# A linear-attention block beside an FFN on one core: kv products in row pairs, smaller first pieces, a split last tile and a new order

## The chip, the cores and the metric

The kernel runs on one core of one Trainium2 chip. The metric is the device time of one execution in microseconds: the median of five runs. Lower is better. Inputs and outputs lie in the chip's main memory and are bf16; products are accumulated in fp32 in PSUM (eight banks).

## The reference

With S = 2048 tokens, D = 448, H = 16 heads of 28 and F = 1792, cut to what matters:

```python
xn = layernorm(x)                                   # A_x; both branches read it
q, k, v = heads(xn @ wqkv)
phi = lambda p: concat(softmax(p), softmax(-p))     # per head, 28 + 28 features
phi_q, phi_k = phi(q @ w_phi), phi(k @ w_phi)
kv = einsum("sf,sd->fd", phi_k, v)                  # per head: sum over all tokens
z  = phi_k.sum(tokens)
o  = (phi_q @ kv) / (phi_q . z + 1e-6)
out = x + merge(o) @ wo + silu(xn @ w1) @ w2
```

## The kernel before

The tokens are cut into 16 tiles of 128. The whole program is recorded first as a list of operations with their data dependencies, and then ordered for each engine by a planner in `schedule()`, from estimated durations and landing times. TensorE's order is nearly written out by hand: the text `PLAN` (from `aF3@4`) fixes the order of its operations from the first chunk of tokens on, and the planner only places the other engines' work and the DMA issues around it. All waits are semaphores that follow from the dependencies.

The work runs in these stages.

- Front. x comes in pieces of one, one, two, four, four and four tiles on SyncE's queue, with pieces of w1 between them (`load_x`, `load_w1`, `load_rows4`). While they come, 38 matmuls on ones keep TensorE busy. `ln_tile(t)` computes mean and variance on DVE, the root of the variance on ACT (tiles 0 to 3) or POOL (later tiles) and the normalised tile `xn` on DVE. Tiles 0 to 3 are transposed by TensorE (`tr0` to `tr3`) and evicted by ACT or DVE; from tile 4 on, two tiles at a time are transposed by a DMA on SyncE's queue (`xnT_dma5`, `xnT_dma7` and so on). The weights of q and k are transposed in the same queue (`wT_dma0` to `wT_dma7`) and multiplied with w_phi on TensorE (`fold_mms`, the words `f2` and `f0` of the plan), so that q and k come out with w_phi applied.
- FFN, first half. `F0` to `F27` are blocks of two 128-row pieces of the hidden layer by 512 tokens; a Silu on ACT evicts two banks at once into `hT`. Blocks 0 to 6 need tiles 0 to 3, blocks 7 to 13 need tiles 4 to 7, and so on. The first three blocks (`head`) are computed tile by tile as the tiles arrive.
- v, k and q blocks of two tiles each. A k or q block has two exponentials on ACT, sums and reciprocals on DVE and a multiply on POOL (`phi_k`, `phi_q`); phi_q is transposed by DMA.
- kv. `kv(ts)` multiplies phi_k with v (and a column of ones for z), head pairs at a time: eight matmuls of 58 columns for each tile, all 16 tiles accumulated in bank 7. `kvm()` masks the result into `KVm` on DVE.
- Attention and output. `U` words multiply phi_q with `KVm`; DVE divides, and a DMA transposes the result. `Y` and `F` words with a count are pieces of the second FFN product (14 matmuls for a tile), `W`, `R`, `r` and `E` add the output projection; `out_ev` adds the residual and sends the tile out.

F, v, k and q blocks have a contraction of 448, which is three and a half times 128. They run in 64-row mode: each matmul uses half of the array's rows, two of them form a pair that writes two banks, and a block has seven pairs. In the plan `a` stands for the first half of a block (three pairs), `b` for the second (four pairs, with the row halves exchanged between the two banks, then the eviction). `@4` is the first of the block's banks. Everything else, kv, fold, U, Y and most of the output projection, uses all 128 rows.

SyncE's queue carries nearly all DMAs in one order, part of which is fixed by `chain(...)`: `wT_dma0` to `wT_dma3`, `xnT_dma5`, `wT_dma4`, `xnT_dma7`, `wT_dma5` to `wT_dma7`, the other token tiles, w2 and wo. The loads of x for tiles 8 to 15 stand before them.

The lines that the change touches most:

```python
pe_mms([(banks[KVB][wide(c), c * 2 * DA:(c + 1) * 2 * DA], ek(t)[:, 0, c * KP:c * KP + wide(c).stop],
         vaug[:, t, 2 * c:2 * c + 2, :]...,
         t == 0 and c == 0, t == NT - 1) for t in ts for c in range(CC)], "kv_mm", ...)
```

Of the kernel before, what the change touches and what calls it, by code (L numbers as in the profile page):

```python
# [140 lines left out]
class _Prog:  # L141
# [68 lines left out]
    def dma(self, fn, xfer, reads=(), writes=(), name="", out_slot=None, eng="sp", issue=480.0, lat=1700.0):  # L210
        o = self.op(eng, issue, fn, reads, writes, name=name)
        o.is_dma = True
        o.xfer = xfer
        o.lat = lat
        o.out_slot = out_slot
        return o

    def schedule(self):
# [21 lines left out]
        eng_free = {e: 800.0 if e == "sp" else 0.0 for e in ENGINES}  # L240
# [93 lines left out]
PLAN = """aF3@4 aF4@0 bF3 aF5@2 av2@6 bF4 bv2 bF5 aF6@0 bF6 av0@4 bv0 aF7@0 aF8@2 aF10@4 bF8 bF10 bF7 f2@26 aF11@4 aF13@0 bF11  # L334
bF13 f0@26 aF9@4 aF12@0 bF9 av4@2 ak0@6 bv4 bF12 bk0 av6@4 av8@2 ak4@0 bv8 bk4 bv6 av14@6 ak2@2 bv14 bk2 av12@0 ak6@4
bv12 bk6 ak8@6 av10@2 ak10@0 bv10 bk10 bk8 ak12@2 ak14@4 bk12 bk14 aq4@0 Y0@6:3 Y0:2 K0-6 bq4 aq6@4 K6-8 bq6 aq0@2 aq8@0
bq0 bq8 aF15@4 Y0:9 K8-12 bF15 aF19@2 aF14@0 bF19 bF14 aF17@5 s4 aF18@3 bF17 bF18 K12-16 aF16@5 aF21@2 aF24@0 bF21 bF16
bF24 M s6 aF27@2 aF26@4 bF27 aF22@0 bF26 bF22 aF20@6 aq2@2 bF20 aF23@0 aF25@4 bF23 bF25 bq2 U4 s8 F4@1:10 U9@0 s0 aq12@6
aq14@4 aq10@2 s2 bq12 bq10 bq14 F4:3 F4:1 F9@0:10 F8@3:3 F8:3 s10 W4 U8 s12 F8:6 Y1@4:14 F9:4 W9 U2 U0@5 F2@2:6 F2:8
F8:2 U7@6 U12@5 W8 Y3@4:9 Y3:5 W2 s14 W0@5 F7@4:9 F7:1 U1 F7:4 W7 R0,2 R8,7 R4,9 F10@6:5 U6@5 U10 F10:9 U3@3 F5@4:14  # L340
U13@2 F15@51:8 U15 F15:6 F12@2:5 F12:9 U14 F6@0:5 W12 E15 U5 F13@3:11 F6:9 F14@7:5 F13:2 F13:1 U11@1 W5 W3@5 r12 W13
F14:9 W14 r14 W6 W1@2 W10 R3,6,13,1,5,10 F11@1:7 F11:6 F11:1 W11 r11"""


def bass_parallel_sum__linear_kernel_hedgehog__dense_activation_silu__prompt_kernel(
# [13 lines left out]
    G = 4  # L359
# [16 lines left out]
    with es:  # L376
# [39 lines left out]
        oT_sb = vflat[:, NO * 512:(NO + NQ) * 512].rearrange("p (n g c) -> p n g c", n=NQ, g=G)  # L416
        KVm = sb("KVm", [KP, CC, 2, DA], BF16)
# [79 lines left out]

        memset(ones_bf[:], 1.0, 128, "ones")
# [6 lines left out]
        act(warm_act[:], ones_bf[:, 0:4], ACTF.Sqrt, 4, "warm_act", table="sqrt")  # L505
# [19 lines left out]
        def load(dst, src, name, eng="sp", lat=1700.0):  # L525
            n = 2
            for _, cnt in list(dst.ap):
                n *= cnt
            P.dma(lambda e: e.dma_start(out=dst, in_=src), n / 280.0, writes=[dst], name=name, eng=eng, lat=lat)  # L529

# [3 lines left out]
        def load_rows4(dst, src, c0, c1, name, lat=1700.0):  # L534
            load(dst[:, 0:3, :], src[0:KF, c0:c1].rearrange("(k p) f -> p k f", p=128), name, lat=lat)
            load(dst[:, 3, :], src[D - 128:D, c0:c1], name, lat=lat)

        def load_w1(c0, c1, lat=1700.0):
            load_rows4(w1_sb[:, :, c0:c1], B_w1, c0, c1, "w1", lat)

        load(Wp[:], A_w_phi.rearrange("(g hl) d f -> (hl d) g f", g=G), "wphi", eng="act", lat=3000.0)
# [3 lines left out]
        load_w1(0, 512)  # L545
        load_w1(512, 1024)
        load_x(4, 8)
        load_w1(1024, FF)
# [8 lines left out]
        def dma_t(dst, src, xfer, name, issue=1235.0, **kw):  # L557
            o = P.dma(lambda e: e.dma_start_transpose(out=dst, in_=src), xfer, lat=650.0, reads=[src] if kw.pop("sbuf", True) else [],
                      writes=[dst], name=name, issue=issue if xfer < 1500.0 else 2000.0, **kw)
            o.crowd = 1  # L560
# [10 lines left out]
        def fold_loads():  # L571
            for a in range(8):
                dma_t(wT_sb[:, a, :], A_wqkv[:, a * KP:a * KP + 128], 600.0, f"wT_dma{a}", (1600.0, 1400.0, 1780.0, 3280.0)[a] if a < 4 else 1300.0, sbuf=False)
# [22 lines left out]
        def ln_tile(t):  # L596
            xs = x_sb[:, t, :]
            sl = t % NXN
            P.op("dve", 590, lambda e: e.bn_stats(st6[:, t, :], xs), reads=[xs], writes=[st6[:, t, :]], name=f"bnst{t}", okeys_w=["ln"])  # L599
            P.op("dve", 170, lambda e: e.bn_aggr(mv[:, t, :], st6[:, t, :]), reads=[st6[:, t, :]], writes=[mv[:, t, :]], name=f"bnag{t}",  # L600
                 okeys_w=["ln"])
            if t < 4:
                P.op("act", 220, lambda e: e.activation(ve[:, t:t + 1], mv[:, t, 1:2], ACTF.Sqrt, bias=epst[:]),
                     reads=[mv[:, t, 1:2], epst[:]], writes=[ve[:, t:t + 1]], name=f"ve{t}", table="sqrt", okeys_r=["sq"])
                P.op("dve", 120, lambda e: e.reciprocal(rstd[:, t:t + 1], ve[:, t:t + 1]),
                     reads=[ve[:, t:t + 1]], writes=[rstd[:, t:t + 1]], name=f"rstd{t}")
            else:
                P.op("pool", 200, lambda e: e.tensor_scalar(ve[:, t:t + 1], mv[:, t, 1:2], EPS_LN, None, ALU.add),
                     reads=[mv[:, t, 1:2]], writes=[ve[:, t:t + 1]], name=f"ve{t}")
                P.op("pool", 570, lambda e: e.tensor_tensor(rstd[:, t:t + 1], ve[:, t:t + 1], neghalf[:], ALU.pow),  # L610
                     reads=[ve[:, t:t + 1], neghalf[:]], writes=[rstd[:, t:t + 1]], name=f"rstd{t}")

            def norm(dst, c0, c1, dur):
                P.op("dve", dur, lambda e: e.tensor_scalar(dst, x_sb[:, t, c0:c1], mv[:, t, 0:1], rstd[:, t:t + 1], ALU.subtract, ALU.mult),  # L614
                     reads=[xs, mv[:, t, 0:1], rstd[:, t:t + 1]], writes=[dst], name=f"xn{t}")

            if t < XN_DMA0:
                norm(xn_sb[:, sl, 0:D], 0, D, 390)
            else:
                norm(xn_sb[:, sl, 0:KF], 0, KF, 370)  # L620
                norm(xn_sb[:, sl, KF:512], D - 128, D, 250)
            dstx = xnT[:, t, :, :]
            if t >= XN_DMA0:
                if t % 2:
                    dma_t(xnT[:, t - 1:t + 1, :, :].rearrange("p i k c -> p (i k) c"),
                          xn_sb[:, sl - 1:sl + 1, :].rearrange("p i c -> p (i c)"), 1300.0, f"xnT_dma{t}", 1350.0)
                return
            tps = bank16[4 + t % 2][:, 0:512].rearrange("p (k c) -> p k c", k=4)
            transposes([(tps[:, kt, :], xn_sb[:, sl, KS[kt]:KS[kt] + 128]) for kt in range(4)], f"tr{t}")
            if t < 3:  # L630
                act(dstx, tps, ACTF.Identity, 512, f"ev{t}")
            else:
                copy(dstx, tps, 512, f"ev{t}")


# [3 lines left out]
        def pair_block(b0, width, lhs, rhs, name):  # L639
            def part(c0, c1):  # L640
                for i in range(2):
                    for n, kt in enumerate((0, 1, 2 + i)):
                        mm(banks[b0 + i][:, c0:c1], lhs(i, kt, slice(0, 128)), rhs(i, kt, slice(0, 128), c0, c1),
                           n == 0 and c0 == 0, False, name)
# [98 lines left out]
        def kv(ts):  # L743
            def wide(c):
# [3 lines left out]
            pe_mms([(banks[KVB][wide(c), c * 2 * DA:(c + 1) * 2 * DA], ek(t)[:, 0, c * KP:c * KP + wide(c).stop],  # L748
                     vaug[:, t, 2 * c:2 * c + 2, :].rearrange("p h c -> p (h c)"),
                     t == 0 and c == 0, t == NT - 1) for t in ts for c in range(CC)], "kv_mm", dur=CC * 30.0 * len(ts), keys_w=["kvbank"])  # L750
# [6 lines left out]
        def phi_q(t, pair=False):  # L757
# [8 lines left out]
            if n % 2 or not pair:  # L766
# [3 lines left out]
                      1300.0 * w, "phqT")  # L770

        def kvm():
            src = banks[KVB][0:KP, 0:2 * DA * CC].rearrange("p (c j e) -> p c j e", c=CC, j=2)
# [9 lines left out]
        def parts(bs):  # L783
            cuts = (0, D) if len(bs) == 1 else (0, 320, D)
# [55 lines left out]
        def out_ev(t, ob, addend, cs):  # L840
# [3 lines left out]
            P.dma(lambda e: e.dma_start(out=outt[:, t, cs], in_=res[:, cs]), 400.0, reads=[res[:, cs]], name="out_dma", out_slot=ob_cnt[0] % NOS,  # L844
# [35 lines left out]
        chain("bnst0 bnag0 bnst1 bnag1 rstd0 xn0 rstd1 xn1 bnst2 bnag2 bnst3 bnag3 rstd2 xn2 rstd3 xn3 ev3".split())  # L880
        chain("ev0 ve2 ev1 ve3 ev2 silu_table".split())
        chain("tr0 tr1 tr2 tr3".split())
# [8 lines left out]
        for t, fs in ((0, head[:2]), (1, head[:2]), (0, head[2:]), (1, head[2:]), (2, head), (3, head)):  # L891
            for f in fs:
                f[0](t * 128, t * 128 + 128)
# [16 lines left out]
        chain("wT_dma0 wT_dma1 wT_dma2 wT_dma3 xnT_dma5 wT_dma4 xnT_dma7 wT_dma5 wT_dma6 wT_dma7 xnT_dma9 xnT_dma11 xnT_dma13 xnT_dma15 w2 "  # L910
              "wo0 wor0 wo1 wor1".split())
        memset(phq[:, :, :, KP:128], 0.0, 400, "phq0")
        late = next(o.id for o in P.ops if o.name == "rstd15")
        ones_column(0, NEK)
        ones_column(NEK, NT)
        for o in P.ops[-2:]:
            o.odeps.add(late)
# [168 lines left out]
```

## Time and profile before

| | |
|---|---|
| median of five runs | 151.43 us (150.49 to 152.01) |
| the profiled execution | 150.49 us |
| its span in the trace | 149.2 us |
| granted TensorE clock | 1.0 in all stages |
| TensorE matmuls | 1412, busy 144.9 us |
| ScalarE (ACT), VectorE (DVE), GpSimd (POOL) busy | 70.1, 91.2, 70.9 us |

A row of the timeline has the start and the length in microseconds, the engine, the line of the kernel, the operation and the number of instructions merged in it. Matmuls are pipelined: the length of a row reaches to the modelled end of its last matmul, so the pace is read from the start of a row to the start of the next. A row of the queue (SPq, ACTq) shows the issue of a DMA, not its transfer; the time from issue to landing is a separate answer of the trace. PEld is the weight load, which overlaps the matmuls.

### The profile page before, as it was taken

To read this page: it belongs to the slowest core of one execution; us is meant where nothing else is said; L and a number is where in the kernel's file an instruction comes from. 1 tells how busy PE (TensorE), PEld (TensorE's weight loads), DVE (VectorE), ACT (ScalarE), POOL (GpSimd) and SP (SyncE) were. 2 spreads that over 40 slices of the span, in tenths; PEclk is the share of its full clock that TensorE was granted. 3 is DMA by queue.
4 is the path that set the end of the run, shared out by engine and by line. 5 is a ranking of instruction groups with operands and counts; after the bars stand their busy time and mean duration, and the time that the engine had idled before them with its cause. 6 is when DMAs were issued, how large, how long until landed. Compare 5 with 4: busy or idle time off the path is not lost.

```text
span 149.2 us, 3394 instructions
## 1 busy us (share of the span) xinstructions
PE 144.9 (97%) x1412; PEld 79.9 (54%) x1412; DVE 91.2 (61%) x186; ACT 70.1 (47%) x86; POOL 70.9 (48%) x82
## 2 busy tenths in 40 slices
PE   7899999999999999999999999999999999999993
PEld 7794435555555565464544445455555567555541
DVE  1958998940098999311995027897552874243354
ACT  3558763557999997975565585910000000000000
POOL 7108568310039999999699900899600000000000
PEclk9999999999999999999999999999999999999999
DMA  5999976999400000000099494078977646240215
GB/s 86 314 373 365 180 131 108 192 237 346 111 0 4 0 0 9 0 4 0 0 76 208 82 185 82 7 136 161 115 155 150 165 120 107 36 100 5 68 67 179
DMA packets 44352, 17.41 MB, mean 117 GB/s; under 512 B 36784, under 2 KB 43952, under 8 KB 44336
## 3 DMA queue, kind: packets, MB, share of 16 engines
q1 hardware_dynamic: 41568, 15.36, 48.4%
q10 hardware_dynamic: 2768, 1.83, 3.8%
q8 instruction: 11, 0.18, 0.5%
q14 instruction: 5, 0.04, 0.1%
HBM read 6.56 MB, written 1.84 MB: 56 GB/s over the span
## 4 chain that ended last, share of the span: by engine, by line
PE 94%; DMA 3%; SPq 1%; issue 0%; DVE 0%
PE psum L468 93%; DMA phT<-in_B_w_dram 3%; SPq L529 1%; DVE x_sb L842 0%; PE psum L483 0%
## 5 line engine op out<-in xcount | busy, mean ns | idle before, releaser
L468 PE MATMUL psum<-xnT,phT 64*128 64x512 bf16 (+1 forms) x428 | 45.2, 350 | 0.7 <-DMA phT<-in_B_w_dram 0.4
L468 PE MATMUL psum<-w_sb,hT 128*128 128x448 bf16 (+1 forms) x238 | 45.4, 342 | 0.0
L488 ACT ACTIVATE hT<-psum 128x1024 bf16<-128x1024 f32 x28 | 27.4, 1023 | 18.5 <-PE psum L468 18.5
L728 DVE TENSOR_REDUCE Rec<-Ek_sb 128x32 f32<-128x896 bf16 (+1 forms) x20 | 24.3, 1246 | 13.7 <-ACT Ek_sb L488 7.9
L468 PEld LDWEIGHTS psum<-xnT,phT 64*128 64x128 bf16 (+1 forms) x428 | 21.2, 95 | 21.4 <-ACT hT L488 0.7
L468 PEld LDWEIGHTS psum<-w_sb,hT 128*128 128x128 bf16 x238 | 21.6, 98 | 19.1 <-issue 1.5
L763 POOL TENSOR_TENSOR RA<-Ek_sb,Rec 128x896 bf16<-128x896 bf16 x16 | 26.6, 1698 | 9.1 <-ACT Ek_sb L488 7.8
L468 PE MATMUL psum<-Wqk,xnT 64*128 64x432 bf16 x224 | 22.9, 343 | 0.0
L488 ACT ACTIVATE Ek_sb<-psum 128x864 bf16<-128x864 f32 x24 | 20.3, 934 | 2.9 <-issue 2.7
L738 POOL TENSOR_TENSOR Ek_sb<-Ek_sb,Rec 128x896 bf16<-128x896 bf16 x8 | 13.3, 1696 | 11.1 <-DVE Rec L729 11.1
L820 DVE TENSOR_SCALAR den<-psum 128x16 f32<-128x16 f32 x16 | 2.5, 160 | 22.3 <-PE psum L468 22.3
L468 PEld LDWEIGHTS psum<-Wqk,xnT 64*128 64x128 bf16 x224 | 10.6, 94 | 9.5 <-ACT Ek_sb L488 0.2
L738 POOL TENSOR_TENSOR phT<-phT,Rec 128x896 bf16<-128x896 bf16 x8 | 13.3, 1693 | 0.0
L468 PE MATMUL psum<-wv,xnT 64*128 64x448 bf16 x112 | 12.9, 350 | 0.1
L599 DVE BATCH_NORM_STATS2 st<-x_sb 128x6 f32<-128x448 bf16 x16 | 9.6, 602 | 4.2 <-DMA x_sb<-in_A_x_dram 4.2
L614 DVE TENSOR_SCALAR RA<-x_sb,mv,rstd 128x384 bf16<-128x384 bf16 (+2 forms) x28 | 10.6, 414 | 1.3 <-POOL rstd L610 1.2
L468 PE MATMUL psum<-wo_sb,vaug 128*128 128x448 bf16 (+2 forms) x51 | 11.0, 342 | 0.0
L827 DVE TENSOR_TENSOR vaug<-psum,rden 128x448 bf16<-128x448 f32 x16 | 9.9, 624 | 0.4
L842 DVE TENSOR_TENSOR x_sb<-psum,x_sb 128x448 bf16<-128x448 f32 (+2 forms) x14 | 7.6, 585 | 3.8 <-PE psum L468 3.8
L729 DVE RECIPROCAL Rec<-Rec 128x32 f32<-128x32 f32 (+1 forms) x24 | 8.5, 390 | 0.1
L468 PEld LDWEIGHTS psum<-wv,xnT 64*128 64x128 bf16 x112 | 5.4, 94 | 5.5 <-PE psum L468 0.5
L488 ACT ACTIVATE vaug<-psum 128x896 bf16<-128x896 f32 x8 | 7.4, 947 | 1.6 <-PE psum L468 1.6
(49 smaller groups left out, 104.1 us busy)
## 6 DMA issues: line engine op xcount, KB each, us to landing
out_dram<-x_sb ACTq DMA_DIRECT2D x15, 112.0 KB, 1.7
w_sb<-in_B_w_dram SPq DMA_DIRECT2D x1, 1568.0 KB, 8.0
x_sb<-in_A_x_dram SPq DMA_DIRECT2D x3, 448.0 KB, 7.8
phT<-in_B_w_dram SPq DMA_DIRECT2D x2, 384.0 KB, 4.7
wo_sb<-in_A_wo_dram SPq DMA_DIRECT2D x2, 336.0 KB, 7.9
phT<-in_B_w_dram SPq DMA_DIRECT2D x1, 576.0 KB, 7.1
wv<-in_A_wqkv_dram SPq DMA_DIRECT2D x1, 336.0 KB, 7.5
phT<-in_B_w_dram SPq DMA_DIRECT2D x2, 128.0 KB, 4.8
```

Of the source, the lines that this page charges most:

```text
L468: r = e.matmul(dst, lhsT, rhs, start=st, stop=sp, skip_group_check=True)
L488: P.op("act", d_act(n), lambda e: e.activation(dst, src, func, scale=scale), reads=[src], writes=[dst], table=table, name=name, **keys)
L529: P.dma(lambda e: e.dma_start(out=dst, in_=src), n / 280.0, writes=[dst], name=name, eng=eng, lat=lat)
L599: P.op("dve", 590, lambda e: e.bn_stats(st6[:, t, :], xs), reads=[xs], writes=[st6[:, t, :]], name=f"bnst{t}", okeys_w=["ln"])
L614: P.op("dve", dur, lambda e: e.tensor_scalar(dst, x_sb[:, t, c0:c1], mv[:, t, 0:1], rstd[:, t:t + 1], ALU.subtract, ALU.mult), reads=[xs, ...
L728: P.op("dve", 50 + 967 * n, lambda e: e.tensor_reduce(R2, E4, AXL.X, ALU.add), reads=[E4], writes=[R2], name="Ssum")
L729: P.op("dve", 135 + 210 * n, lambda e: e.reciprocal(R2, R2), reads=[R2], writes=[R2], name="Rrec")
L738: P.op("pool", 1700, lambda e: e.tensor_tensor(E3, E3, Rk[:, :, None].broadcast_to([128, 32, DH]), ALU.mult), reads=[E3, Rk], writes=[E3], ...
L763: P.op("pool", 1700, lambda e: e.tensor_tensor(dst, Eq, Rq.rearrange("p (c j) -> p c j", c=CC)[:, :, :, None].broadcast_to([128, CC, 4, DH ...
L820: P.op("dve", 190, lambda e: e.tensor_scalar(den[:, uq, :], U3[:, :, DH], EPS_DEN, None, ALU.add), reads=[U3[:, :, DH]], writes=[den[:, uq ...
L827: P.op("dve", 620, lambda e: e.tensor_tensor(o3, U3[:, :, 0:DH], rden[:, uq, :, None].broadcast_to([128, H, DH]), ALU.mult), reads=[U3[:, ...
L842: P.op("dve", d_dve(cs.stop - cs.start), lambda e: e.tensor_tensor(res[:, cs], ob, addend[:, cs], ALU.add), reads=[ob, addend[:, cs]], wri ...
```

## The change

- kv: each matmul of 128 rows becomes two of 64 rows. The low half accumulates in bank 7, the high half in bank 6. `kvm()` gains two steps before the mask: ACT copies bank 6 into `kvsum`, DVE adds bank 7 to it; the mask then reads `kvsum`.
- First loads: w1's first piece has 256 columns in place of 512; its pieces for columns 256 to 767 are issued on ACT's queue behind the table load, and the rest on SyncE's queue is cut anew. The load of x for tiles 12 to 15 moves behind `xnT_dma5`; `wT_dma3` and `wT_dma4` move behind `xnT_dma7`.
- Tile 0: normalised, transposed and evicted in two halves (256 and 192 columns). The first blocks are ordered piece by piece.
- Last tile: the split of its two column parts is 224 and 224 in place of 320 and 128, and tile 15 is now the very last one (`F15@61:14 E15` ends the plan).
- `PLAN` is a new order. It starts with both halves of F3, block 12 is the first one that needs tiles 4 to 7, Y2 comes in one piece among the v and k blocks, and kv comes in groups of 4, 4, 2, 2 and 4 tiles. Estimates of issue and transfer times in the planner's calls change with it.
- The columns of ones in `Ek` are set after the last normalised tile instead of after its reciprocal root.

```diff
-PLAN = """aF3@4 aF4@0 bF3 aF5@2 av2@6 bF4 bv2 bF5 aF6@0 bF6 av0@4 bv0 aF7@0 aF8@2 aF10@4 bF8 bF10 bF7 f2@26 ...
+PLAN = """aF3@4 bF3 aF6@0 aF4@2 bF6 av2@4 bF4 av0@6 bv2 bv0 aF12@0 aF8@2 aF9@4 bF8 bF9 aF11@6 bF12 bF11 f2@24 ...
...
         load_x(0, 1)
         load_x(1, 2)
         load_x(2, 4)
-        load_w1(0, 512)
-        load_w1(512, 1024)
+        load_w1(0, 256)
+        load(w1_sb[:, 3, 256:768], B_w1[D - 128:D, 256:768], "w1_256r")
+        for c in (256, 512):
+            load(w1_sb[:, 0:3, c:c + 256], B_w1[0:KF, c:c + 256].rearrange("(k p) f -> p k f", p=128), f"w1_{c}", "act")
         load_x(4, 8)
-        load_w1(1024, FF)
+        load_w1(768, 1280)
+        load_w1(1280, FF)
...
+            if t == 0:
+                norm(xn_sb[:, sl, 0:256], 0, 256, 290, "a")
+                norm(xn_sb[:, sl, 256:D], 256, D, 275)
+                turn_over(0, 2, 4, "0a")
+                turn_over(2, 4, 5, "0")
...
-            pe_mms([(banks[KVB][wide(c), c * 2 * DA:(c + 1) * 2 * DA], ek(t)[:, 0, c * KP:c * KP + wide(c).stop],
-                     vaug[:, t, 2 * c:2 * c + 2, :].rearrange("p h c -> p (h c)"),
-                     t == 0 and c == 0, t == NT - 1) for t in ts for c in range(CC)], "kv_mm", dur=CC * 30.0 * len(ts), keys_w=["kvbank"])
+            pe_mms([(banks[KVB - i][wide(c), c * 2 * DA:(c + 1) * 2 * DA], ek(t)[r, 0, c * KP:c * KP + wide(c).stop],
+                     vaug[r, t, 2 * c:2 * c + 2, :].rearrange("p h c -> p (h c)"),
+                     t == 0 and c == 0, t == NT - 1) for t in ts for c in range(CC) for i, r in enumerate((LOW, HIGH))],
+                   "kv_mm", dur=CC * 30.0 * len(ts), keys_w=["kvbank"], mode=64, tiles=(KVB, KVB - 1))
...
         def kvm():
-            src = banks[KVB][0:KP, 0:2 * DA * CC].rearrange("p (c j e) -> p c j e", c=CC, j=2)
+            lo, hi = (banks[KVB - i][0:KP, 0:2 * DA * CC] for i in range(2))
+            P.op("act", d_act(464), lambda e: e.activation(kvsum[:], hi, ACTF.Identity), reads=[hi], writes=[kvsum[:]], name="kvhi")
+            P.op("dve", d_dve(464), lambda e: e.tensor_tensor(kvsum[:], lo, kvsum[:], ALU.add), reads=[lo, kvsum[:]], writes=[kvsum[:]], name="kvsum")
+            src = kvsum[:].rearrange("p (c j e) -> p c j e", c=CC, j=2)
...
-            cuts = (0, D) if len(bs) == 1 else (0, 320, D)
+            cuts = (0, D) if len(bs) == 1 else (0, D // 2, D)
...
-        chain("wT_dma0 wT_dma1 wT_dma2 wT_dma3 xnT_dma5 wT_dma4 xnT_dma7 wT_dma5 wT_dma6 wT_dma7 xnT_dma9 ...
+        chain("x8 wT_dma0 wT_dma1 wT_dma2 xnT_dma5 x12 xnT_dma7 wT_dma3 wT_dma4 wT_dma5 wT_dma6 wT_dma7 xnT_dma9 ...
...
-        late = next(o.id for o in P.ops if o.name == "rstd15")
+        late = max(o.id for o in P.ops if o.name == "xn15")
...
-            o.odeps.add(late)
+            o.deps.add(late)
```

## The prediction

> **What bounds the kernel now.** First the page: its busy table and its chain say which engine sets the end.
>
> ```profile
> span 149.2 us, 3394 instructions
> PE 144.9 (97%) x1412; PEld 79.9 (54%) x1412; DVE 91.2 (61%) x186; ACT 70.1 (47%) x86; POOL 70.9 (48%) x82
> PE 94%; DMA 3%; SPq 1%; issue 0%; DVE 0%
> ```
>
> TensorE is the path. A busy share can still hide slow packing, so next the chain of waits in order of time (start, length, what):
>
> ```profile
> 2.19 4.44 DMA phT<-in_B_w_dram
> ...
> 21.66 0.20 issue
> 21.85 124.98 PE psum L468 x1196
> 146.83 0.02 issue
> 146.85 0.62 DVE x_sb L842
> ```
>
> So the chain has a DMA-bound front (first useful matmul at 6.77), 125 us of unbroken matmuls, and a tail. Nothing on DVE, ACT or POOL can gain anything by itself from 22 to 147 us; only what TensorE executes, and what starts and ends its row, counts. Then the timeline of PE gives the unit prices (start, length; I read one start minus the one before, since ends overlap):
>
> ```profile
> 30.52 0.96 PE L468 MATMUL psum<-BDphi,Y_sb 112*128 112x112 bf16 x16
> 31.41 2.33 PE L468 MATMUL psum<-xnT,phT 64*128 64x512 bf16 x20
> ...
> 54.20 1.67 PE L468 MATMUL psum<-vaug,Ek_sb 128*128 128x58 bf16 x48
> 55.80 1.45 PE L468 MATMUL psum<-Wqk,xnT 64*128 64x432 bf16 x14
> 57.18 0.67 PE L468 MATMUL psum<-vaug,Ek_sb 128*128 128x58 bf16 x16
> 57.79 3.46 PE L468 MATMUL psum<-Wqk,xnT 64*128 64x432 bf16 x36
> ...
> 83.03 4.05 PE L468 MATMUL psum<-xnT,phT 64*128 64x512 bf16 x36
> 86.91 0.89 PE L468 MATMUL psum<-Wqk,xnT 64*128 64x432 bf16 x8
> ```
>
> 36 matmuls of 512 columns in 64-row mode take 86.91-83.03 = 3.88 us: 18 pairs of 0.2156 us. Two row halves cost what one matmul of 512 columns must cost at full clock, so halves run side by side. A 448-column pair is 0.189, a 432-column pair 0.183, a 128-column matmul 0.056. The kv products: 48 in 1.60 us and 16 in 0.61 us, each including one exit into 64-row mode. A mode switch: 16 fold products of 112 columns take 0.89 with their exit, 0.79 without by the same rate (0.0493 each): 0.10 us a switch. So kv is about 0.031 us per matmul, 4.0 us for all 128.
>
> **1. The front, to the first fold.** Tile 0 is normalised, transposed and evicted in two halves; w1's first piece shrinks from 512 to 256 columns, and two pieces go to ACT's queue. Before, the first matmul needed w1 (landed 2.19+4.44 = 6.63) and tile 0's eviction (5.98+0.60 = 6.58). After, x tiles 2-3 (224 KB, issued 1.73, landing 3.9 later at 5.6) still stand ahead of w1; half of the old piece should land half way from 5.6 to 6.63, 6.1. The transposes of tile 1 still come first in PE order, and DVE now spends about 0.15 more on tile 0 (two pieces in place of one of 0.40; a 128-column piece has 0.31 and overlaps its neighbour by 0.08), so tile 1's transposes end near 6.25. Start 6.3: 0.45 earlier. ACT's two issues (0.4 each) fit between its warm-up (ends 2.75) and its first variance (4.10): hidden; ACT-queue pieces share the DMA engines, and for a second piece that lands late I allow 0.15 of stalls.
>
> What follows is the same work in both orders until the first fold: 7 FFN blocks (7 pairs x 0.2156 = 1.51 each) and 2 v blocks (7 x 0.189 = 1.32). Before, this stretch also held four stalls: 0.11 (tile 2's eviction), 0.20 (a Silu that frees banks 0-1), 0.22 twice where a block's two halves are adjacent and the swapped row half must write the bank just left (F6, v0), and 0.36 where F7 waits for the transposed tokens of tiles 6-7:
>
> ```profile
> 19.93 1.73 PE L468 MATMUL psum<-wv,xnT 64*128 64x448 bf16 x14
> 21.85 4.71 PE L468 MATMUL psum<-xnT,phT 64*128 64x512 bf16 x42 [0.20 <-issue]
> 26.49 0.96 PE L468 MATMUL psum<-BDphi,Y_sb 112*128 112x112 bf16 x16
> ```
>
> (14 matmuls are 7 x 0.189 = 1.32; they take 1.92: 0.22 + 0.36 and rounding.) The SP queue explains the 0.36: xnT_dma7 issues at 18.05 and lands 3.7 later, 21.75.
>
> ```profile
> 8.73 6.60 SPq L558 DMA_TRANSPOSE Y_sb<-in_A_wqkv_dram  x4
> 15.37 1.32 SPq L558 DMA_TRANSPOSE xnT<-RA  x1
> 16.73 1.27 SPq L558 DMA_TRANSPOSE Y_sb<-in_A_wqkv_dram  x1
> 18.05 1.31 SPq L558 DMA_TRANSPOSE xnT<-RA  x1
> 19.39 4.21 SPq L558 DMA_TRANSPOSE Y_sb<-in_A_wqkv_dram  x3
> ```
>
> The new order keeps one adjacent pair here (F3, 0.22), loses the Silu wait, and asks for tiles 4-7 one block earlier (F12 comes after five blocks, F7 came after six). Count: stall-free front 26.49-6.77-1.12 = 18.6; 6.3+18.6+0.22+0.15 = 25.3 at the fold; F12 lies 4 x 1.51 = 6.04 and a switch before it, so F12 wants its tokens at 19.15. On SP, two weight transposes (1.3 us of issue each) move behind xnT_dma7, a load of x (0.7 of issue, 448 KB) moves in front of it from before wT0. The fourth transpose is held until about 15 (the fourth took 2.6 us of issue before); then 0.7 for x, xnT_dma7 at about 16.0, landing 3.7 later: 19.7 (19.1 to 20.5). F12 then waits 0.55, and the fold starts at 25.9. The fold has a second gate: the last weight transpose is again the tenth on SP, issued at about 22.35 and landing 3.5 later, 25.85. Both agree on 25.9: -0.6 us (+0.2 to -0.9). So most of a faster head is eaten by transposes behind it; what is late next is xnT_dma7, then wT_dma7.
>
> **2. One more adjacent pair** later: k2's halves follow each other, +0.22, none before there.
>
> **3. Mode switches.** The instruction order has 20 changes between 64-row and full mode before and 14 after: before, the order leaves 64-row mode four times for kv (twice with a piece of Y0 beside it), after once, for Y2 whole. 3 returns less, two switches each: 6 x 0.095 = -0.56.
>
> **4. kv itself.** 128 matmuls become 128 pairs. No row shows a 58-column pair. From below: as one full matmul, or a hair less, -0.1 in all. From above: the two halves one after the other, 0.060 a pair, +3.7. Nearest row: the 512-column pairs at the price of one. Against it speaks the Trainium skill: "TensorE: Matmul & The Clock Gate" (Wait — 56ns, not 53.3ns?) gives a start-to-start floor of about 25 ns per matmul however few its columns, and "TensorEngine Tiling (Array Packing)" (Instruction Overhead) advises against taking a tiling factor from a dimension already that small. By that rule 256 matmuls cost at least 6.4 instead of 4.0: +2.4. The 512-column rows say the floor doesn't hold between the two row halves, but at 216 ns a pair they leave issue ample time; at 29 ns four instructions must be issued where two are now. I take 0.032 a pair: +0.1.
>
> **5. New evacuation.** kvhi (ACT) and kvsum (DVE, as kvm 0.58) come before kvm. kvm ended at 80.5, the first U is at 87.7: 7 us of cover; ACT idles 1-3 us between Silus there. Behind kvhi on ACT stands a Silu that frees FFN banks; 0.5 late is within the two-block distance. Cost 0; without cover about 1.2. Moving the ones columns behind xn15 ends the 2.5 us that two normalise instructions took beside POOL's memset at 25.1; the fold subtraction waited for ACT's fold_ref there, so 0.
>
> **6. The tail.** Before: last matmul 0.35, DVE 0.62, DMA 1.7. After, the last half has 224 columns: matmul about 0.26 (0.22 at 128, 0.30 at 320), DVE 0.38 (0.28 and 0.49), DMA 1.63 (halves landed 1.6 after issue). -0.37. Two 224s cost as one 448 on PE: 320+128 already do.
>
> Elsewhere I walked the new order with these durations against ACT (exp pair 1.7, v 0.9), POOL (1.66 per phi) and the bank releases: every wait keeps at least about 0.2 us, as the old order does.
>
> Sum: -0.6+0.22-0.56+0.1+0-0.37 = -1.2. The profiled execution took 150.49 (1.3 outside its span), giving 149.3; it was the fastest of five, 0.94 under the median 151.43. Against the median: **150.2**.
>
> **The rivals.**
> *A, kv pairs do not overlap (slower).* One mechanism: in 58-column pairs the issue of four instructions, or one shared weight load, sets the pace. Break-even is 1.2/128 = 0.009 above 0.032: from about 0.041 us a pair the change loses, from 0.047 by over 0.5%. At 0.050 150.2+2.3 = 152.5; fully serial 153.8. For: the floor above, and 58-column matmuls already cost 31 and not the 24 ns of their columns. Against: 2 starts per pair in every 64-row row without extra. 22%.
> *B, the front gains nothing (no change).* xnT_dma7 lands at 20.5 or later, because the x load in front of it takes its 1.2 us on busy DMA engines: fold at 26.6, then +0.1 in place of -0.6, 150.9; with kv at 0.035 another 0.4. 15%.
> *C, an unforeseen wait in the new order* (a phi multiply or oT transpose late on SP by 1 to 2 us): 151.5 to 152.3. 5%.
> The forecast has 58%.
>
> **How the numbers follow.** 0.5% is 0.76 us, about what a measurement can tell from no change. Forecast's own range 149.5 to 150.7; B reaches 151.3, A's lower half to 153.0. Range 149.4 to 153.0 leaves out full serialisation and luck. Faster 0.58, same 0.16 (B and the forecast's upper edge), slower 0.26 (A, C).
>
> **What would show it.** First L469 matmul of xnT near 6.3; F12 after a gap near 19.7; fold near 25.9; 64 kv matmuls in one group in about 1.0 us with no 0.1 us at its edges; the last DVE row 0.38. If kv groups take 1.6 to 2 us for 64 matmuls, A is right; if the fold stays at 26.5, B.

## The result, and the profile after

| | before | after |
|---|---|---|
| median | 151.49 us (150.25 to 152.52, 43 runs) | 150.07 us (149.51 to 151.95, 22 runs) |
| ratio after/before | | 0.9926, 95% interval 0.9904 to 0.9948 |
| the profiled execution | 150.49 us, span 149.2 | 150.27 us, span 149.0 |

The kernel became faster, by 0.7% (0.5 to 1.0%); the forecast was 150.2 us. (The ratio leaves disturbed runs out, so it is not quite the quotient of the medians.) The two profiles differ by only 0.2 us, though, and that is where the study starts. First the page of after: its span and its busy table.

```profile
span 149.0 us, 3651 instructions
PE 143.7 (96%) x1540; PEld 80.2 (54%) x1540; DVE 90.7 (61%) x189; ACT 71.3 (48%) x88; POOL 71.4 (48%) x82
```

TensorE has 128 matmuls more and is busy 1.2 us less; it still sets the end. The chain of waits (start, length, what) has the same form as before: a front that ends with a DMA, TensorE without a break from block F12 on, a tail.

```profile
2.20 5.12 DMA phT<-in_B_w_dram
7.32 0.05 issue
7.36 1.51 PE psum L469 x24
...
20.18 0.74 issue
20.92 14.83 PE psum L469 x150
...
35.79 110.84 PE psum L469 x1184
...
146.66 0.77 DVE x_sb L856 x2
```

Two things here are not as forecast: w1's first piece lands at 7.32 and not at 6.1, so the first useful matmul is at 7.36 (before: 6.77), and F12 starts at 20.92 and not at 19.7. The timeline of PE gives the rest: the first fold product, and the five groups of kv products (the start of the row after a group ends it).

```profile
27.07 0.96 PE L469 MATMUL psum<-BDphi,Y_sb 112*128 112x112 bf16 x16
...
56.83 1.16 PE L469 MATMUL psum<-vaug,Ek_sb 64*128 64x58 bf16 x64
57.83 2.35 PE L469 MATMUL psum<-Wqk,xnT 64*128 64x432 bf16 x24
...
60.39 1.16 PE L469 MATMUL psum<-vaug,Ek_sb 64*128 64x58 bf16 x64
61.39 1.44 PE L469 MATMUL psum<-Wqk,xnT 64*128 64x432 bf16 x14
...
65.55 0.66 PE L469 MATMUL psum<-vaug,phT 64*128 64x58 bf16 x32
66.05 1.67 PE L469 MATMUL psum<-xnT,phT 64*128 64x512 bf16 x14
67.56 0.66 PE L469 MATMUL psum<-vaug,phT 64*128 64x58 bf16 x32
68.06 1.67 PE L469 MATMUL psum<-xnT,phT 64*128 64x512 bf16 x14
69.57 1.17 PE L469 MATMUL psum<-vaug,phT 64*128 64x58 bf16 x64
70.58 1.67 PE L469 MATMUL psum<-xnT,phT 64*128 64x512 bf16 x14
```

64 matmuls (32 pairs) take 57.83-56.83 = 1.00 us: 0.031 us a pair, what one full-row matmul took before. All five groups are 1.00+1.00+0.50+0.50+1.01 = 4.01 us; before they were 4.41 with four exits of about 0.095, that is 4.03. Rival A is refuted.

**The fold splits the time cleanly.** From the first fold product to the end of the span it is 149.2-26.49 = 122.7 us before and 149.0-27.07 = 121.9 after: 0.8 us less behind the fold. Ahead of it, after is 27.07-26.49 = 0.6 *later* in these two profiles. The span of a typical execution says otherwise. If the stretch behind the fold is constant, the median of before (a span of 151.49-1.29 = 150.2) has its fold at 27.5, and that of after (150.07-1.27 = 148.8) at 26.9: 0.6 earlier. So either the profile of before shows an untypically early fold, or the stretch behind it varies. The first experiment asks that.

### The profile page after: what moved, and what is told of

It reads as the page before. It is cut to its first block, busy times and chain, and to the rows that moved or that the text cites. A ratio compares the mean times of both kernels' runs of the same rounds, so it can differ in the third digit from the quotient of the medians.

```text
span 149.0 us, 3651 instructions
## 1 busy us (share of the span) xinstructions
PE 143.7 (96%) x1540; PEld 80.2 (54%) x1540; DVE 90.7 (61%) x189; ACT 71.3 (48%) x88; POOL 71.4 (48%) x82
## 4 chain that ended last, share of the span: by engine, by line
PE 93%; DMA 3%; SPq 1%; issue 1%; DVE 1%
PE psum L469 93%; DMA phT<-in_B_w_dram 3%; SPq L503 1%; DVE x_sb L856 1%; PE psum L484 0%
## 5 line engine op out<-in xcount | busy, mean ns | idle before, releaser
L774 POOL TENSOR_TENSOR RA<-Ek_sb,Rec 128x896 bf16<-128x896 bf16 x16 | 27.1, 1722 | 11.5 <-DVE Rec L739 11.5
L469 PEld LDWEIGHTS psum<-w_sb,hT 128*128 128x128 bf16 x238 | 22.2, 98 | 18.3 <-issue 1.5
L834 DVE TENSOR_SCALAR den<-psum 128x16 f32<-128x16 f32 x16 | 2.6, 161 | 19.7 <-PE psum L469 19.6
L856 DVE TENSOR_TENSOR x_sb<-psum,x_sb 128x448 bf16<-128x448 f32 (+1 forms) x13 | 7.1, 582 | 9.6 <-PE psum L469 9.6
L469 PE MATMUL psum<-wv,xnT 64*128 64x448 bf16 x112 | 12.4, 349 | 0.0
L469 PE MATMUL psum<-wo_sb,vaug 128*128 128x448 bf16 (+1 forms) x51 | 10.7, 342 | 0.0
L618 DVE TENSOR_SCALAR RA<-x_sb,mv,rstd 128x384 bf16<-128x384 bf16 (+4 forms) x29 | 8.9, 343 | 1.3 <-POOL rstd L614 1.2
L738 DVE TENSOR_REDUCE Rec<-phT 128x64 f32<-128x1792 bf16 x4 | 7.9, 1987 | 2.6 <-ACT phT L489 2.6
```

The source lines that it names most:

```text
L469: r = e.matmul(dst, lhsT, rhs, start=st, stop=sp, skip_group_check=True)
L738: P.op("dve", 50 + 967 * n, lambda e: e.tensor_reduce(R2, E4, AXL.X, ALU.add), reads=[E4], writes=[R2], name="Ssum")
L774: P.op("pool", 1700, lambda e: e.tensor_tensor(dst, Eq, Rq.rearrange("p (c j) -> p c j", c=CC)[:, :, :, None].broadcast_to([128, CC, 4, DH ...
L834: P.op("dve", 190, lambda e: e.tensor_scalar(den[:, uq, :], U3[:, :, DH], EPS_DEN, None, ALU.add), reads=[U3[:, :, DH]], writes=[den[:, uq ...
L856: P.op("dve", d_dve(cs.stop - cs.start), lambda e: e.tensor_tensor(res[:, cs], ob, addend[:, cs], ALU.add), reads=[ob, addend[:, cs]], wri ...
```

## The experiments

**b1_look and b2_look: two more profiles of before.** No edit.

> The kernel before, unchanged, profiled a second time, because the profile of it shown first was one of its fastest executions (150.49 us against a median of 151.4). Theory A, the transfers of the head land differently from execution to execution: the span here is 149.5 to 150.5 us, the first useful matmul or the start of block F7 (after xnT_dma7) is later than the 6.77 and the 21.8 us of the first profile by what the span is longer, and the stretch from F7's start to the last matmul is again 124.98 us within 0.15. Theory B, the rest of the kernel varies: the head is the same within 0.2 us and the stretch from F7 on is 0.5 us or more longer. If the span is 149.2 again, neither is told apart by this look.

> The kernel before, unchanged, a third profile of it, for the same question as b1_look. Theory A: span 149.5 to 150.5 us with the surplus ahead of F7's start. Theory B: the surplus behind it, in the stretch of 124.98 us.

They took 151.08 and 151.34 us, spans 149.8 and 150.1. The chain of waits around F7, of b1_look and then of b2_look:

```profile
21.53 0.94 issue
22.47 124.98 PE psum L468 x1196
```

```profile
21.87 0.86 issue
22.73 124.98 PE psum L468 x1196
```

124.98 us for the third time, to the last digit: theory A. All of the surplus lies ahead of F7, which starts 0.62 and 0.88 us later than in the first profile. Most of it is the wait for the DMA-transposed tiles 6 and 7, 0.94 and 0.86 us where the first profile had 0.20 (in b1_look and b2_look `xnT_dma7` landed 4.2 us after its issue, in the first profile 3.7). The folds are at 27.11 and 27.37. So the first profile was a lucky one, in these profiles the spread from run to run arises ahead of the fold, and "time behind the fold is constant" may be used to read a front off a span.

**e1_kv_full: kv back to full rows.** One bank, no `kvhi`, no `kvsum`; all else as in after.

```diff
-                    vaug[r, t, ...]... for t in ts for c in range(CC) for i, r in enumerate((LOW, HIGH))],
-                   "kv_mm", ..., mode=64, tiles=(KVB, KVB - 1))
+                    vaug[:, t, ...]... for t in ts for c in range(CC)], "kv_mm", ...)
```

> The changed kernel with the kv products back in full-row mode in one bank (no kvhi, no kvsum); all else, the order too, as changed. Theory (switches): its five kv groups stand between 64-row blocks, so 10 more mode switches of 0.095 us, and 128 matmuls of 0.031 in place of pairs that the trace of after shows at about 0.031: the fold-to-end stretch is 0.95 us longer, time 150.07 + 0.95 = 151.0, ratio to before about 0.998. Rival (the pairs cost more than they save in switches, the gain lies elsewhere): equal to or faster than the changed kernel, 150.1 or less.

Measured: 151.28 us, ratio 1.0007 to before (0.9976 to 1.0039): all of the gain is gone. The timeline of its PE and the end of its chain:

```profile
57.54 1.18 PE L469 MATMUL psum<-vaug,Ek_sb 128*128 128x58 bf16 x32
58.65 2.73 PE L469 MATMUL psum<-Wqk,xnT 64*128 64x432 bf16 x28
61.31 1.18 PE L469 MATMUL psum<-vaug,Ek_sb 128*128 128x58 bf16 x32
```

```profile
36.41 111.90 PE psum L469 x1056
```

32 products take 1.11 us with their exit where after took 1.00, and the 14 pairs between two groups 61.31-58.65 = 2.66 where 14 x 0.183 = 2.56 are work: 0.10 to 0.11 for each switch of mode. Five groups make ten switches, and the unbroken stretch is 111.90-110.84 = 1.06 us longer. The row pairs are worth this, not less work: in the new order every kv group stands among 64-row blocks. (The median lost 1.21; part of the rest is the granted clock, under e7_fill.)

**e2_old_loads: w1 loaded as before**, 512 columns first, all on SyncE's queue.

```diff
-        load_w1(0, 256)
-        load(w1_sb[:, 3, 256:768], ..., "w1_256r")
-        for c in (256, 512):
-            load(w1_sb[:, 0:3, c:c + 256], ..., f"w1_{c}", "act")
+        load_w1(0, 512)
+        load_w1(512, 1024)
```

> The changed kernel with the first loads of w1 back as before (512 columns first, all on SyncE's queue, none on ACT's). Theory (the pieces on ACT's queue issue at 1.31, ahead of the piece that is needed first, and slow it): first matmul back at about 6.7 instead of 7.36; the stall at block 12 grows by the same amount since the transposed tokens land at about 20.8 either way, fold unchanged near 27.0: time within 0.2 us of the changed kernel (150.1). Rival (the new loads bring the gain): 0.5 us or more slower than the changed kernel, 150.6 or more.

Measured: 149.84 us, 0.9906 (0.9871 to 0.9941). In its profile the old 512-column piece landed at 6.48, earlier than the new 256-column piece in after (7.32), and the fold began at 26.48. The rival, 150.6 or more, is refuted: the new loads bring nothing that can be seen here. The theory comes near in the time (150.1 within 0.2) but not in the way to it. It had F12's stall grow as much as the first block gained, with the fold near 27.0; the first block started 0.75 us earlier than in after, the stall grew by 0.09 (to 0.83), and the fold came 0.6 earlier, because `xnT_dma7` landed at 20.24 and not at 20.8. The rows of ACT in after show how the new loads delay the needed piece:

```profile
1.25 1.28 ACT L489 ACT_TABLE_LOAD   x1 [1.25 <-PEq L1093]
1.31 0.99 ACTq L503 DMA_DIRECT2D phT<-in_B_w_dram  x2
```

The two pieces on ACT's queue are issued at 1.31 and 1.80, during the table load and not behind it as the list of changes has it, and so ahead of the piece that the first block needs, which is issued on SyncE at 2.20. They landed at 4.48 and 6.95, x tiles 2 and 3 at 6.22 (before: 5.59), the needed piece at 7.32. In the four profiles with these loads (after, e1, e3, e7) the needed piece landed at 7.00 to 7.32; in the six with the old loads (before, b1_look, b2_look, e2, e9, e10) the old one, twice as large, at 6.05 to 6.82.

**e4_first_piece_act: the needed piece first.** Piece 0:256 goes to ACT's queue, 256:768 to SyncE's.

```diff
-        load_w1(0, 256)
-        ... "w1_256r"; "w1_256" and "w1_512" on "act"
+        load(w1_sb[:, 0:3, 0:256], ..., "w1_0", "act")
+        load(w1_sb[:, 3, 0:768], ..., "w1_0r")
+        load(w1_sb[:, 0:3, 256:768], ..., "w1_256")
```

> The changed kernel with the first w1 piece (columns 0 to 255) on ACT's queue, so that it is issued at 1.3, and the other early pieces on SyncE's queue behind x. Theory A (the time is set behind the front by the token transpose for block 12 at 20.8 and the weight transposes): first matmul at about 6.2 in place of 7.36, stall at block 12 longer by 1.1, fold within 0.2 us of 27.0, time 150.0 to 150.2. Theory B (the front counts in full): first matmul 1.1 earlier and the end 1.1 earlier, 149.0. Theory C (an idle TensorE before the first block lowers the granted clock in a part of the runs): the gap of 1.3 us before the first block shrinks to under 0.3, and no run has a granted clock of 0.989; the median falls toward the fast group of the changed kernel's runs, 149.8.

Measured: 149.59 us, 0.9883 (0.9850 to 0.9915). The start of its first block, the fold, and the chain at F12:

```profile
6.29 1.94 PE L469 MATMUL psum<-xnT,phT 128*128 128x128 bf16 x24
...
26.05 0.96 PE L469 MATMUL psum<-BDphi,Y_sb 112*128 112x112 bf16 x16
```

```profile
7.00 0.05 issue
7.05 1.18 PE psum L469 x18
...
19.53 0.37 issue
19.90 14.83 PE psum L469 x150
```

The times are those that the prediction had drawn: first matmul 6.29 (forecast 6.3), F12 at 19.90 (19.7), fold at 26.05 (25.9). The first matmul is 1.07 earlier than in after's profile, the fold and the end 1.02. That does not show that a gain at the first matmul arrives at the end, though. Behind six matmuls the first blocks stop until 7.05, when `w1_256` (landed 7.00) is there, and F12 still waits 0.37 us, for `xnT_dma7`: it landed at 19.81 here and at 20.83 in after. Whether the moved piece brought that is open, as e5 shows. The median is 0.5 under after's, but the ratios' intervals overlap, and it is none that the three theories named.

**e5_first_block_act: its remainder rows too.** e4 with `w1_0r` (0:256) on ACT's queue as well.

> The kernel after with both pieces of w1 that the first block needs (256 columns of the three whole row groups, and 256 of the remainder) on ACT's queue, ahead of everything on it but w_phi, and the other pieces on SP. Theory B (the head counts in full: what block F12's start gains, the end gains): the first block runs without the stall of 0.43 us that e4 showed in front of its remainder rows; F12 still waits for xnT_dma7, so only a part of the 0.43 arrives: span 147.6 to 148.0, median 149.2 to 149.6. Theory C (xnT_dma7's landing alone sets F12): span as e4's 148.0 within 0.15 and median 149.6 within 0.2. Theory A (the head is hidden behind the fold): median 150.0.

Measured: 149.75 us, 0.9930 (0.9906 to 0.9954), no better than e4: inside theory C's range for the median, while its span of 149.1 lies outside what any theory named. The experiment rests on a misreading. e4's stall was not in front of the remainder rows, which had landed at 5.96, but in front of `w1_256`, the whole row groups of the next piece. Here that piece landed at 7.63, and the wait is longer:

```profile
7.68 1.18 PE L469 MATMUL psum<-xnT,phT 128*128 128x128 bf16 x18 [1.01 <-DMA phT<-in_B_w_dram]
```

`xnT_dma7` landed at 20.87, F12 started at 20.96 and the fold at 27.11; the span is again the fold plus 122.0. Beside after, e2, e4 and e3 (below; its front is after's):

| | first matmul | x of tiles 8 to 11 landed | `xnT_dma7` landed | F12 starts |
|---|---|---|---|---|
| after | 7.36 | 15.50 | 20.83 | 20.92 |
| e3_whole_tail | 7.29 | 14.97 | 20.25 | 20.34 |
| e2_old_loads | 6.61 | 15.04 | 20.24 | 20.33 |
| e4_first_piece_act | 6.29 | 14.54 | 19.81 | 19.90 |
| e5_first_block_act | 6.17 | 15.65 | 20.87 | 20.96 |

F12 starts 0.09 us behind the landing of `xnT_dma7` in all five, and waits for it in all five (0.24 to 0.83 us), wherever the first matmul stood: the earliest first matmul (e5) has the latest F12. So in these profiles a faster head by itself *is* eaten, as the prediction said and as theory C has it. The landing follows that of x for tiles 8 to 11 by 5.2 to 5.3 us, and it differs by 0.6 us between after and e3, which have the same front. Whether an order of w1's pieces moves it cannot be told from one profile of each.

**e6_x12_later, e8_both, e9_old_loads_x12: x for tiles 12 to 15 behind `xnT_dma7`.** One line, put on e5, e4 and e2 in turn.

```diff
-        chain("... xnT_dma5 x12 xnT_dma7 wT_dma3 ...")
+        chain("... xnT_dma5 xnT_dma7 x12 wT_dma3 ...")
```

> e5 with the last x load, x12, issued on SP behind xnT_dma7 instead of ahead of it, so that xnT_dma7 is issued about 0.5 us earlier. Theory C (xnT_dma7's landing alone sets F12's start): F12 starts 0.3 to 0.4 us earlier than in e5, its wait of 0.37 us is gone, and the end follows: span 147.3 to 147.6, median 149.0 to 149.3. Theory D (the next gate takes it over: x12 and the four transposes of w_qkv that follow it land later, so tiles 12 to 15 or the fold wait): a new wait of 0.2 to 0.5 us in front of the fold or of a transpose of tile 12, and the median is e5's or up to 0.3 above it.

> e4 (first piece of w1 on ACT's queue, all else as in after) with x12 issued behind xnT_dma7. Theory B (the head counts in full up to the next gate): e4's wait of 0.37 us in front of block F12 goes; F12 starts near 19.5; of the 0.37 a part comes back in front of the fold, as e6 showed 0.21 us there: span 147.7 to 148.0 (e4's profile had 148.0), median 149.2 to 149.5. Theory D (the fold's gate takes all of it): e4's median 149.6 within 0.15, with a wait in front of the fold of 0.35 us or more.

> e2 (the loads of w1 as in the kernel before, all on SP) with x12 issued behind xnT_dma7. Theory B: e2's wait of 0.83 us in front of block F12 goes or falls under 0.2 us, F12 starts at 19.5 to 19.7, and 0.2 to 0.4 us comes back in front of the fold: span 147.8 to 148.1 (e2's profile had 148.4), median 149.2 to 149.6. Theory D (the fold's gate takes all of it): median 149.84 within 0.2. If the loads of w1 on ACT's queue were worth something behind the first block, this is slower than e6 (149.41) by more than 0.3 us.

Measured: e6 149.41 us, 0.9902 (0.9866 to 0.9939); e8 149.88, 0.9941 (0.9907 to 0.9976); e9 149.95, 0.9922 (0.9887 to 0.9957). All three lose the wait in front of F12, which starts at 19.71, 19.44 and 19.57. Their folds, in the timeline of e6, of e8 and of e9:

```profile
26.13 0.95 PE L469 MATMUL psum<-BDphi,Y_sb 112*128 112x112 bf16 x16 [0.21 <-ACT hT L489]
```

```profile
26.41 0.95 PE L469 MATMUL psum<-BDphi,Y_sb 112*128 112x112 bf16 x16 [0.77 <-DMA Y_sb<-in_A_wqkv_dram]
```

```profile
26.59 0.95 PE L469 MATMUL psum<-BDphi,Y_sb 112*128 112x112 bf16 x16 [0.82 <-DMA Y_sb<-in_A_wqkv_dram]
```

0.37 us saved at F12 against e4, and 0.77 spent at the fold; 0.83 against e2, and 0.82. In the profiles this is theory D: the last weight transpose, the tenth on SyncE's queue, is the second gate, and it stands so close behind the first that moving one load past `xnT_dma7` gives nothing that can be seen. The load in front of `xnT_dma7` does cost what rival B of the prediction feared: with it there, the transpose landed 4.4 to 4.6 us after its issue (after and e1 to e5; 6.2 in e7's late front), with it behind, 3.1 (e6, e8, e9). e6 came through with 0.21: its last weight transpose landed at 25.99, those of e8 and e9 at 26.28 and 26.45, and each fold starts 0.13 to 0.14 us after that. In the medians only e9 is inside theory D's range; e8's 149.88 is above both of its ranges, and e6's 149.41 lies between its two. e9 is slower than e6 by 0.54 in the median, more than the 0.3 set beforehand for "the loads on ACT's queue are worth something", but they ran beside different runs of before and their ratios agree within the intervals: not settled.

**e10_before_order: before, with SyncE's order of after.** Two weight transposes moved behind `xnT_dma7`, nothing else.

```diff
-        chain("wT_dma0 wT_dma1 wT_dma2 wT_dma3 xnT_dma5 wT_dma4 xnT_dma7 wT_dma5 ...")
+        chain("wT_dma0 wT_dma1 wT_dma2 xnT_dma5 xnT_dma7 wT_dma3 wT_dma4 wT_dma5 ...")
```

> The kernel before with one line changed: two of the weight transposes, wT_dma3 and wT_dma4, are issued on SP behind xnT_dma7, as the kernel after does it; plan, loads, kv and tail stay as before. Theory S (the head's part of the gain comes from SP's order of transposes alone): xnT_dma7 lands before 21.5 us, the wait in front of block F7 (0.20, 0.94 and 0.86 us in the three profiles of before) goes, the fold starts at 26.3 to 26.6 us (26.49, 27.11 and 27.37 before), the stretch from the fold to the end of the span stays 122.7 us, so the span is 149.0 to 149.3 and the median 0.5 to 1.0 us under that of before run beside it. Theory W (the second gate, wT_dma7, is as late as the first one typically is): a wait of 0.4 us or more in front of the fold takes the place of F7's, the fold starts at 26.8 or later and the median is within 0.4 us of before.

Measured: 151.06 us against 151.16 for before beside it, 0.9985 (0.9950 to 1.0021): no difference, theory W. Its profile is of a slower execution than most (151.95 us). In the PE timeline F7 no longer waits (21.69), and the fold does:

```profile
21.69 4.70 PE L468 MATMUL psum<-xnT,phT 64*128 64x512 bf16 x42
28.00 0.95 PE L468 MATMUL psum<-BDphi,Y_sb 112*128 112x112 bf16 x16 [1.61 <-DMA Y_sb<-in_A_wqkv_dram]
```

The chain of waits shows what held the queue (in order of time; L599 and L600 are the statistics of a tile, L614 its normalisation):

```profile
6.94 9.40 DMA x_sb<-in_A_x_dram
...
16.36 0.64 DVE st L599
...
18.45 0.29 DVE RA L614
18.74 0.16 SPq L558
...
24.96 2.69 DMA Y_sb<-in_A_wqkv_dram
...
28.00 120.33 PE psum L468 x1154
```

In this execution DVE waits for x of tiles 8 to 11 until 16.34 (15.0 to 15.3 in the three profiles of before), and behind their statistics stands the last piece of tile 7's normalisation, which `xnT_dma7` needs. While that transpose waits on SyncE, the five weight transposes wait behind it, and the last of them lands at 27.65. How long the fold waits in a typical execution is not known from this; the median says that SyncE's order alone does not give the front its 0.6 us. (120.33 us from the fold to the last matmul is before's own 124.98 less the 4.64 from F7 to the fold.)

**e3_whole_tail: the last tile in one piece.**

```diff
-... F15@61:14 E15"""
+... F15@6:14 E15"""
```

> The changed kernel with tile 15, still last, in one piece of 448 columns. Theory (the split shortens the chain behind the last matmul): DVE 0.62 in place of 0.38 and a last matmul of 0.35 in place of 0.26, landing of 112 KB 0.04 later: 0.37 us longer, 150.4. Rival (TensorE pays for twice the matmuls, 28 of 224 columns, what DVE saves): no difference within 0.1 us.

Measured: 150.84 us, 0.9978 (0.9951 to 1.0005). The end of its chain:

```profile
35.22 111.18 PE psum L469 x1170
146.40 0.02 issue
146.42 0.62 DVE x_sb L856
```

From its fold (26.50) to the end of the span (148.80) it is 122.30 us against 121.95 in after: the split is worth 0.35 us, and the rival is refuted. The median says 0.8; the granted clock accounts for the rest, as the next experiment shows.

**e7_fill: twelve matmuls on ones in the gap** between tile 1's transposes and the first block. The reason: 4 of 23 executions of after, the profiled one counted, had a mean granted clock of 0.989 and took 151.2 to 152.0 us; all others had 1.0 and took 150.8 at most. e1 had 4 such executions of 14, e3 4 of 22. The row of the granted clock in e1's page, 40 slices of 3.8 us in tenths of full speed, shows where:

```profile
PEclk9959999999999999999999999999999999999999
```

A slice at 0.5: its first block took 2.64 us where after's 24 matmuls took 1.51. In the trace itself the clock is 0.50 from 7.19 to 10.60, 3.41 us, with the matmuls 0.107 us apart and not 0.056; in the 3.41 us ahead of that TensorE was busy for 1.92. These executions also explain what the medians had left over: among those at 1.0 alone, e3's median is 150.30 against after's 149.91, 0.4 as in the traces, and e1's 151.06 is 1.15 over after's, near the 1.06 of its trace.

> The kernel after with 12 matmuls of 128x128 on a tile of ones (into a bank that nobody reads yet) placed on PE between tile 1's transposes and the first block, that is, into the gap of 1.05 to 1.27 us in which PE waits for w1_0. Theory P (the runs of after whose mean granted clock is 0.989 come from a half-speed stretch that this idle gap brings on): no run at 0.989, where after had 4 of 23 and e1 and e3, with the same gap, 4 of 14 and 4 of 22; the runs from 150.8 up vanish, median 149.7 to 150.0. Theory Q (the low clock has nothing to do with the gap): about one run in five at 0.989 again, and the median 150.1 to 150.4. In both, the filler takes 0.7 to 1.3 us of the gap, so the first block starts at most 0.2 us later than it would, and since the wait for xnT_dma7 lies behind it, the span of a run at full clock is after's within 0.2 us.

Measured: 150.09 us, 0.9923 (0.9885 to 0.9960), and 2 of 12 executions at 0.989, one of them the profiled one, whose front came late (x for tiles 8 to 11 landed at 16.02). In it the gap is filled and the first block runs at full clock; the low stretch, again 3.41 us (23.52 to 26.94), comes at F12, behind a wait:

```profile
22.97 1.39 PE L469 MATMUL psum<-xnT,phT 64*128 64x512 bf16 x8 [2.98 <-DMA xnT<-RA]
```

Theory P said that no run would be at 0.989, so it fell as it was stated. (Its two took 154.0 and 154.2 us, far above after's four; none like those four came, but 0 of 12 against 4 of 23 can be chance.) That the low clock follows *some* idle stretch of TensorE fits both profiles and isn't shown. The Trainium skill ("TensorE: Matmul & The Clock Gate", What's actually happening) has the clock set to half or full by windows of about 3.4 us that run on regardless of the kernel. The length agrees, 3.41 us in both profiles; so does the chance from run to run. But it asks for a whole idle window, and in the 3.41 us ahead of the low stretch TensorE was busy for 1.92 us in e1 and 0.55 in e7. The kernels whose needed piece comes early (e2, e4, e5, e6, e8, e9) had no such run in 64, and the kernel before, run beside the experiments and as e10, 3 in 120.

## Why the prediction was right, and where its steps were not

**Right sum.** 1.2 us were forecast against the median; the medians differ by 1.4, the ratio says 1.1. Behind the fold this was earned, ahead of it partly luck.

**Behind the fold, forecast -0.61, measured -0.76** (122.71 us before, 121.95 after). The form of this sum held:

- One more adjacent pair (k2), forecast +0.22: 36.53-35.02 = 1.51 us for 14 matmuls that take 42.85-41.57 = 1.28 where the halves are apart, so +0.23.

```profile
35.02 1.68 PE L469 MATMUL psum<-Wqk,xnT 64*128 64x432 bf16 x14
36.53 0.73 PE L469 MATMUL psum<-wv,xnT 64*128 64x448 bf16 x6
...
41.57 1.44 PE L469 MATMUL psum<-Wqk,xnT 64*128 64x432 bf16 x14
42.85 0.92 PE L469 MATMUL psum<-wv,xnT 64*128 64x448 bf16 x8
```

- Six switches fewer, forecast -0.56 at 0.095: e1's ten switches cost 1.06, so about 0.106 each, and -0.63.
- kv, forecast +0.1 (0.032 a pair): 4.01 against 4.03, so 0. The rule of the Trainium skill that was weighed here ("TensorE: Matmul & The Clock Gate", the 25 ns from start to start) would have 256 matmuls take 6.4 us, and they took 4.0: it does not hold between the two row halves. It would have turned the sign; the row of 512-column pairs was the better guide. The other rule weighed there, on a dimension that is already small, does not bear on this change: the factor of two was taken from the 128 rows, not from the 58 columns. Another section of the page on the clock gate was the one to weigh ("Measured speedup vs the span model"): it counts about 4 ns of issue for each further tile of a packed group. The trace agrees: the two matmuls of a kv pair start 2 to 4 ns apart, and the next pair mostly 22 to 27 ns after that.
- `kvhi` and `kvsum`, forecast 0 because first U is far: the masked result is there at 80.2, the first U is at 88.5. Eight microseconds of cover.
- Tail, forecast -0.37: e3 measured 0.35.

With the measured sizes: +0.23-0.63-0.02-0.35 = -0.77, where the spans show -0.76.

**Ahead of the fold, forecast -0.6: right in the medians, by errors that cancel, and that is luck.** The count of the work held: from the first matmul to the fold, less F12's wait, after takes 27.07-7.36-0.74 = 18.97 us, which is the forecast 18.6+0.22+0.15. "Most of a faster head is eaten by transposes behind it" held too, for `xnT_dma7` (the table under e5) and for `wT_dma7` close behind it (e8, e9 and e10). The steps that failed:

- "Half of the old piece should land half way from 5.6 to 6.63, 6.1": it landed at 7.32. The prediction counted the two issues on ACT as hidden because ACT has room for them, and allowed them 0.15 us of stalls. It did not ask when they are issued against the piece that is needed, though it says itself that they share the DMA engines. This put the first matmul 1.06 us late. What that costs at the end is not shown: in after's profile F12 would have had to wait for `xnT_dma7` all the same, if that landed no earlier.
- "xnT_dma7 at about 16.0, landing 3.7 later: 19.7": issued at 16.21, it landed 4.62 later, at 20.83. The 3.7 was read from before, where no load of x is issued right in front of it. With that load in front it took 4.4 us or more in every profile, with the load behind it 3.1 (e6, e8, e9). This is the step that put F12 and the fold about a microsecond late in after's profile.
- The profile of before was taken as a typical front and its total shifted to the median. It was not: F7 waits 0.2 us in it and 0.9 in the two others, and the typical fold is at 27.1 to 27.5, not 26.5. So before's fold was taken a microsecond too early as well, and the difference survived.

**Rival B** (the front gains nothing) looks true in the first pair of profiles and is false in the medians. Its mechanism came about, though: `xnT_dma7` landed at 20.83, "20.5 or later", because of the load in front of it. Only the typical front of before was late too. Neither w1's new loads (e2) nor SyncE's order of transposes (e10) gives the 0.6 us alone. The place of the load of x for tiles 12 to 15, the two halves of tile 0 and the new plan of the first blocks remain; they were not tried apart, and which of them carries it stays open.

No variant is shown to beat after: e4 has the lowest ratio, 0.9883, with an interval that overlaps after's, and e8, its nearest relative, had 0.9941.

## What to carry to other kernels

Find the instant from which the bound engine never waits again (here the first fold product) and split both profiles there: behind it the time repeats to 0.1 us and single terms of 0.2 us can be read, ahead of it two executions of one kernel differ by 0.9 us and one profile is a sample of one. When a load is moved to another queue, ask when it is issued against the load that is needed first, not whether the queue's engine has time; and a landing time read from one order of a queue is not that of another. An earlier start is worth something only if the next gate moves with it: put the gate's landing beside the start in every profile. Row pairs can be worth using for small products even where they save no time in themselves, if what stands around them runs in row pairs too, as here.

## What the runs showed of the hardware

- Two 64-row matmuls of 58 columns on the two row halves took 0.031 us together, as one of 128 rows does; four instructions (two weight loads, two matmuls) in place of two did not slow them.
- Each switch between 64-row and full-row mode cost about 0.106 us in e1, entries as well as exits.
- DMAs issued on ACT's queue did not wait for ACT's table load: it ran from 1.25 to 2.53, and they were issued at 1.31 and 1.80.
- A DMA transpose issued right behind a load of 448 KB landed 4.4 to 4.6 us after its issue in six profiles (6.2 in a seventh), with the load behind it 3.1 in three.
- In some executions the granted clock fell to half for one stretch of 3.41 us within the front, which cost e1's first block 1.1 us. TensorE had been busy for 1.92 us of the 3.41 ahead of it in e1, for 0.55 in e7; what brings it on is not settled.
- A mean granted clock of 1.0 leaves out the first climb: in every profile the matmuls at the start are 0.107 us apart (half speed), in after until 4.6 us, in before until 6.0, in e4 until 6.6.
